# Letting a main product be issued up to ten places ahead of the first unissued one

## The chip, the cores and the metric

The program runs on one core of a Trainium2 chip. The metric is the device time of one execution in microseconds (us), the median of several. Below, PE is the matrix engine (TensorE), DVE the vector engine, ACT the scalar engine, POOL the general engine (GpSimd) and SP the engine whose queue issues all the DMAs here. Matmuls read SBUF and write PSUM, which here is eight banks of 128 partitions by 512 floats.

## The reference

Three layers in a row, all in float32, on 4 batches of 768 tokens (3072 tokens in all).

```python
# attention: 4 batches, 8 heads, 768 tokens, head size 64
scores = scale * np.matmul(q, k.transpose(0, 1, 3, 2))
keep = is_global | is_local            # 8 global keys, and the 96 keys up to the query's own
scores = np.where(keep, scores + bias, -1000000000.0)
a = exp(scores - max); a = a / (sum(a) + 1e-09)
x = (a @ v) as [3072, 512]
# layer 1: w_in [512, 2048], w_out [2048, 512]
h = x @ w_in;  x = (h * np.cos(h)) @ w_out
# layer 2: weights of the same shapes
h = np.maximum(x @ w_in, 0.0);  return h * h @ w_out
```

## The kernel before

**Tiling.** The 3072 tokens are cut into six blocks of 512 (`b` = 0 to 5), each of four tiles of 128 tokens. Every float32 operand of a large product is split into two float16 parts, high and low, and a product is the sum of three float16 products (`PRODS`). Attention goes tile by tile (`attend32` for the first four tiles, `attend` for the others), in two groups of four heads: scores (`scores_and_bias`, or bias by DVE for the last tiles), maximum, exponential, a transpose of the probabilities by DMA, and `values`, whose sums DVE divides (line 929) into `x`.

**The main products.** Layer 1 of a block is 16 steps `j`. `first(b, j)` (line 1038) multiplies the block's `x` with a 128-column part of `w_in` into one PSUM bank, 12 matmuls of 512 columns. `hidden` (ACT and DVE) turns the bank into the pair of halves `g` that `second(b, j)` (line 1056) multiplies with a row part of `w_out`, again 12 matmuls, added up over `j` in four other banks. Layer 2 is done with seven instead of eight products of quarters (`product`, line 1148: the names P1 to P7, 12 matmuls of 256 columns each), then `tokens` (line 1350) for blocks 0 to 2 and `second2` (line 1270) for blocks 3 to 5; for the latter `token_quarters` prepares the quarters. All these go through one helper, `pe` (line 1032). The PSUM banks are two pools of four: `h` for `first`, for P1 to P7, for the scores and for `values`; `yp` for the sums of `second`, `tokens` and `second2`.

**Weights.** They come as raw 64-bit words, 1 MB at a time, for two steps `j` each. `decoded` (line 486) turns them into float32 by one ACT and three DVE operations, `weight` (line 498) splits them, the low half on DVE or POOL (line 409). While block 0 is in layer 1 its weights are still being decoded, `w_in` and `w_out` in turn.

**The order of the work.** Nothing is issued by hand. Every piece of work is a `Work` object in a `Plan` with a cost in us, a due time, the buffers that it takes, and the pieces that it depends on. `order` first hands due times down: a piece is due no later than 0.01 us before each piece that depends on it. `run` then plays a clock: whenever an engine is free, it takes the piece with the earliest due time among those whose dependences are done and whose buffers can be had (`can_get`, which keeps buffers back for pieces that are due earlier). The result is one fixed list for each engine; on the chip each engine issues its list in that order and waits where an operand or a buffer is late.

**The row.** `pe` ties each main product to the one before it in the order in which the program writes them down: the predecessor is in `after`, so a main product isn't ready in the planner until its predecessor is done, whatever its own operands. That order is, in layer 1, `first(b, j)` followed by `second` of three steps earlier (`LAG = 3`), across the border of blocks too; in layer 2 the P products with `tokens` or `second2` between them (`fill`). The scores, the values and the norms of attention are added by `plan.add` directly and aren't in the row.

Of the kernel before, what the change touches and what calls it, by code (L numbers as in the profile page):

```python
# [79 lines left out]
SLACK = 0.8  # L80
SWITCH = 10.0
AHEAD_OF = 6
ROUNDS = 1


class Buf:
    def __init__(self, pool):
        self.pool, self.slot, self.users, self.writers, self.readers = pool, None, [], [], []
# [10 lines left out]
class Plan:  # L99
    def __init__(self, pools):  # L100
        self.free = {k: list(range(n)) for k, n in pools.items()}
        self.work = []

    def add(self, ways, due, emit, r=(), w=(), new=(), part=(), after=(), lag=0.1, tab=None):

# [25 lines left out]

    def order(self):

        for o in reversed(self.work):
            for d in o.deps:
                d.due = min(d.due, o.due - 0.01)
        for o in self.work:
            for d in sorted(o.deps, key=lambda d: d.n):
                d.outs.append(o)
        best = None  # L140
        self.ends = []
        for n in range(ROUNDS):
            try:
                started = self.run()
            except RuntimeError:
                if best is None:
                    raise
                break
            self.ends.append(round(self.end, 1))
            if best is None or self.end < best[0]:  # L150
                bufs = {b: b.slot for o in started for b in o.gets}
                best = self.end, started, [(o.start, o.end, o.eng) for o in started], bufs, self.switches
            self.relax(started, n)
        self.end, started, placed, bufs, self.switches = best
        for o, (o.start, o.end, o.eng) in zip(started, placed):
            pass
        for b, b.slot in bufs.items():
            pass
        return started
# [32 lines left out]
    def run(self):  # L192
# [4 lines left out]
        for o in work:  # L197
            o.left, o.eng = len(o.deps), None
            for b in o.bufs:
                users[b] = len(b.users)  # L200
        lines = {k: [] for k in pools}
        for o in sorted(work, key=lambda o: (o.due, o.n)):
            for b in o.gets:
                lines[b.pool].append(o)
# [4 lines left out]
        port_until, port_by, bus, table = 0.0, None, 0.0, "exp"  # L209
        events, now, done = [], 0.0, 0  # L210
# [11 lines left out]
        def can_get(o):  # L222
            need = {}
            for b in o.gets:
                need[b.pool] = need.get(b.pool, 0) + 1
            for p, k in need.items():
                line, i = lines[p], at[p]
                while line[i].eng is not None:
                    i += 1
                at[p] = i  # L230
                kept, seen = 0, 0
                while line[i] is not o:
                    if line[i].eng is None:
                        kept += 1
                        seen += 1
                        if seen > AHEAD_OF:
                            return False
                    i += 1
                if len(pools[p]) < k + kept:
                    return False  # L240
                if o.ways[0][0] == "SP" and pools[p][k - 1][0] > now + 1e-9:
                    return False
            return True

        while done < len(work):
            moved = True
            while moved:
                moved = False
                for e in engines:
                    if free_at[e] > now + 1e-9:  # L250
                        continue
                    if e == "SP" and bus > now + AHEAD:
                        seq += 1
                        heapq.heappush(events, (bus - AHEAD, 3, seq, None, None))
                        continue
                    held, pick, key = [], None, 0.0
                    beside = e == "DVE" and self.waits_for_pool(ready, free_at, now)
                    while ready[e]:
                        item = heapq.heappop(ready[e])
                        o = item[2]  # L260
                        if o.eng is not None:
                            continue
                        way = next(w for w in o.ways if w[0] == e)
                        port = way[2]
                        ok = can_get(o) and not (port and port_until > now + 1e-9 and port_by != e)
                        if ok and e == "POOL" and len(o.ways) > 1:
                            ok = self.pool_may(o, now, free_at, ready)
                        if ok and e == "ACT":
                            k = o.due + (SWITCH if o.tab not in (None, table) else 0.0)
                            if pick is None or k < key:  # L270
                                pick, key = (o, way), k
                            if key <= o.due:
                                held.append(item)
                                break
                        elif ok and e == "DVE":
                            k = o.due + (SHARED if len(o.ways) > 1 else 0.0) + (BESIDE if port and beside else 0.0)
                            if pick is None or k < key:
                                pick, key = (o, way), k
                            if key <= o.due:
                                held.append(item)  # L280
                                break
                        elif ok:
                            pick = (o, way)
                            break
                        held.append(item)
                        if len(held) > 60:
                            break
                    for item in held:
                        if pick is None or item[2] is not pick[0]:
                            heapq.heappush(ready[e], item)  # L290
                    if not pick:
                        continue
                    o, way = pick
                    o.eng, o.start = e, now
                    for b in o.gets:
                        b.slot = pools[b.pool].pop(0)[1]
                    if e == "SP":
                        issue, xfer = way[1]
                        end_issue = now + issue
                        bus = max(bus, end_issue) + xfer  # L300
                        end = bus + 1.8
                        free_at[e] = end_issue
                    else:
                        end = free_at[e] = now + way[1]
                        if e == "ACT" and o.tab not in (None, table):
                            table, end = o.tab, end + 1.3
                            free_at[e] = end
                            self.switches += 1
                        if way[2]:
                            port_until, port_by = end, e  # L310
                    o.end = end
                    seq += 1
                    heapq.heappush(events, (end + o.lag, 0, seq, o, None))
                    heapq.heappush(events, (free_at[e], 2, seq, None, None))
                    for x in o.outs:
                        same = e != "SP" and len(x.ways) == 1 and x.ways[0][0] == e
                        seq += 1
                        heapq.heappush(events, (end if same else end + o.lag, 1, seq, o, x))
                    started.append(o)
                    moved = True  # L320
# [8 lines left out]
            now = events[0][0]  # L329
            while events and events[0][0] <= now + 1e-9:  # L330
                _, kind, _, o, x = heapq.heappop(events)
# [29 lines left out]
def fast_path(ctx, tc, kq, vt, w, n_raw, out, meanwhile):  # L361
# [32 lines left out]
    plan = Plan({k: len(v) for k, v in slots.items()})  # L394
# [69 lines left out]
    start, now = {}, T0  # L464
# [14 lines left out]
    def unit_due(m, b, e, j):  # L479
        step = LEN[m, b] / (2 * NJ)  # L480
        return start[m, b] + (2 * j + 5 * e) * step
# [545 lines left out]


    yd = {}
    last_pe = [None]  # L1030

    def pe(due, us, fn, **k):

        o = plan.add((("PE", us, False),), due, fn, after=[last_pe[0]] if last_pe[0] else (), lag=0.3, **k)
        last_pe[0] = o
        return o

    def first(b, j, due):
# [540 lines left out]
    for m, b in SEQ:  # L1579
# [17 lines left out]
        for j in range(0 if m or b in SEVEN else NJ):  # L1597
            due = unit_due(0, b, 0, j)
# [11 lines left out]
        for q in range(0 if m or b not in SEVEN else NQ):  # L1610
            due = start[0, b] + q * LEN[0, b] / NQ
# [7 lines left out]
        for q in range(NQ if m else 0):  # L1619
            due = start[1, b] + q * LEN[1, b] / NQ  # L1620
# [257 lines left out]
```

## Time and profile before

| | us |
|---|---|
| median of 3 runs | 1136.92 |
| lowest and highest run | 1131.3 and 1138.05 |
| the profiled execution | 1133.71 |
| its span, first to last instruction | 1132.0 |
| PE busy in it | 1082.7 (96%) |
| DVE busy | 743.7 (66%) |
| ACT busy | 743.4 (66%) |
| POOL busy | 155.2 (14%) |
| mean granted clock of TensorE | 0.986 of full |

The span is a little shorter than the device time. Busy time counts an instruction from start to end; matmuls overlap one another by a little, so that a listed duration of 12 matmuls is longer than their share of a dense stream. A bracket behind a row, as `[1.58 <-DVE x L929]`, is the idle time of the engine before that instruction and what ended it.

### The profile page before, as it was taken

Reading aid. Unit: us, or ns where it says so; the run is one execution under the profiler, and the core shown is the slowest. Engines: PE = TensorE matmul, PEld = TensorE weight load, DVE = VectorE, ACT = ScalarE, POOL = GpSimd, SP = SyncE. Lnnn points to the kernel's source line nnn. Section 1 sums busy time; section 2 is a strip of 40 time slices with the busy share of each in tenths; the row PEclk is TensorE's granted clock in tenths of the full one; section 3 lists DMA queues with packets and bytes.
Section 4 is the critical chain, followed back from the end, with each engine's and each line's share of the span. In section 5 each row is a group of like instructions: output and inputs, shape, how many; then the busy total and the mean of one; then the engine's idle time right before and its main releaser. Section 6 shows DMA issues by size and latency. Waiting matters only on the chain.

```text
span 1132.0 us, 21315 instructions
## 1 busy us (share of the span) xinstructions
PE 1082.7 (96%) x8612; PEld 677.2 (60%) x8612; DVE 743.7 (66%) x1347; ACT 743.4 (66%) x1283; POOL 155.2 (14%) x125
## 2 busy tenths in 40 slices
PE   6898899989999999999999999999999999999997
PEld 5744444544455444666666554666544588888886
DVE  6998887569777975575554564455683277477473
ACT  6979767688999663775754865674554377376361
POOL 0211220012121210120000110000140032022010
PEclk9988989999999999999999999999999999999999
DMA  5576779449787873588786624586873363334201
GB/s 214 196 216 169 243 248 290 124 85 258 226 209 185 301 272 112 194 262 234 224 204 237 184 94 93 141 219 185 331 263 137 121 224 112 128 126 149 77 9 41
DMA packets 151979, 207.65 MB, mean 183 GB/s; under 512 B 103808, under 2 KB 104320, under 8 KB 150336
## 3 DMA queue, kind: packets, MB, share of 16 engines
q1 hardware_dynamic: 151872, 206.21, 60.0%
q8 instruction: 69, 1.13, 0.4%
q14 instruction: 38, 0.31, 0.1%
HBM read 149.03 MB, written 32.51 MB: 160 GB/s over the span
## 4 chain that ended last, share of the span: by engine, by line
PE 83%; DVE 10%; ACT 4%; DMA 1%; issue 1%; SPq 0%; POOL 0%; DVEq 0%; ACTq 0%; POOLq 0%
PE hps L1047 20%; PE ypps L1063 19%; PE hps L1154 18%; PE ypps L1360 11%; PE ypps L1290 7%; PE hps L912 2%; DVE nm L807 2%; PE hps L1290 2%; PE hps L851 1%; DVE dec L65 1%; DMA raw<-w 1%; ACT L815 1%; ACT e L815 1%; DVE p L409 1%; PE hps L1487 1%
## 5 line engine op out<-in xcount | busy, mean ns | idle before, releaser
L1047 PE MATMUL hps<-xy,w 128*128 128x512 f16 x1152 | 273.4, 388 | 10.5 <-ACT e L815 3.2
L1063 PE MATMUL ypps<-g,ld 128*128 128x512 f16 x1152 | 264.6, 379 | 0.6 <-issue 0.4
L1154 PEld LDWEIGHTS <-ld 128*128 128x128 f16 x2016 | 196.1, 98 | 35.5 <-issue 4.0
L1047 PEld LDWEIGHTS <-w 128*128 128x128 f16 x1152 | 111.9, 99 | 146.3 <-issue 17.2
L1154 PE MATMUL hps<-ys,ld 128*128 128x256 f16 x1680 | 196.4, 273 | 1.4 <-ACT t L1390 1.4
L1063 PEld LDWEIGHTS <-ld 128*128 128x128 f16 x1152 | 112.6, 98 | 135.3 <-issue 1.7
L409 DVE TENSOR_TENSOR g<-t,g 128x512 f16<-128x512 f32 x142 | 109.3, 771 | 50.3 <-ACT g L1131 49.7
L1348 DVE TENSOR_TENSOR t<-hps,t 128x512 f32<-128x512 f32 x120 | 82.7, 689 | 88.9 <-PE hps L1154 87.9
L1360 PE MATMUL ypps<-ld,g 128*128 128x512 f16 x576 | 133.2, 379 | 0.0
L1087 DVE SCALAR_TENSOR_TENSOR t<-t,hps 128x512 f32<-128x512 f32 x96 | 65.6, 683 | 87.2 <-ACT t L1085 87.0
L1131 ACT ACTIVATE g<-t 128x512 f16<-128x512 f32 x144 | 90.0, 625 | 39.9 <-DVE t L1087 38.4
L1083 ACT ACTIVATE t<-hps 128x512 f32<-128x512 f32 x96 | 57.1, 594 | 86.4 <-PE hps L1047 83.7
L1360 PEld LDWEIGHTS <-g 128*128 128x128 f16 x576 | 55.8, 98 | 57.6
L1345 ACT ACTIVATE t<-t 128x512 f32<-128x512 f32 x72 | 45.0, 625 | 61.5 <-DVE t L1348 61.4
L1085 ACT ACTIVATE t<-t 128x512 f32<-128x512 f32 x96 | 60.4, 629 | 2.7
L1180 ACT ACTIVATE t<-t 128x512 f32<-128x512 f32 x96 | 60.3, 629 | 2.6
L409 DVE TENSOR_TENSOR p<-e,p 128x1024 f16<-128x1024 f32 (+1 forms) x32 | 37.3, 1167 | 31.0 <-ACT p L899 30.9
L1345 ACT ACTIVATE t<-hps 128x512 f32<-128x512 f32 x24 | 14.3, 597 | 50.4 <-PE hps L1154 50.3
L875 DVE CUSTOM_DVE_ANT_0 e<-hps,bias 128x256 f32<-128x256 f32 (+2 forms) x96 | 31.7, 387 | 18.4 <-PE hps L851 18.3
L883 ACT ACTIVATE e<-e,nm 128x256 f32<-128x256 f32 (+1 forms) x96 | 39.1, 477 | 3.6 <-DVE nm L875 3.5
L65 DVE SCALAR_TENSOR_TENSOR dec<-raw,dec 128x1024 int32<-128x1024 int32 x32 | 40.3, 1258 | 0.6
L409 POOL TENSOR_TENSOR kq<-ld,kq 128x1024 f16<-128x1024 f32 x9 | 19.9, 2211 | 149.9 <-ACT kq L628 149.9
(193 smaller groups left out, 1515.7 us busy)
## 6 DMA issues: line engine op xcount, KB each, us to landing
ld<-w SPq DMA_DIRECT2D x146, 512.0 KB, 4.2
raw<-w SPq DMA_DIRECT2D x32, 1024.0 KB, 5.5
w<-ld SPq DMA_DIRECT2D x36, 512.0 KB, 3.0
ld<-kq SPq DMA_DIRECT2D x23, 512.0 KB, 5.2
ld<-vt SPq DMA_DIRECT2D x24, 256.0 KB, 3.3
yd<-xy SPq DMA_DIRECT2D x6, 1024.0 KB, 6.1
xy<-yd SPq DMA_DIRECT2D x6, 1024.0 KB, 5.6
ld<-w SPq DMA_DIRECT2D x24, 256.0 KB, 3.6
```

The source lines that it names most:

```text
L409: op.emit = lambda: eng[op.eng].tensor_tensor(out=out_f(), in0=src_f(), in1=hi_f(), op=ALU.subtract)
L1047: nc.tensor.matmul(out=at(ps), lhsT=w_view(wt)[:, a, j % 2, k * 128:(k + 1) * 128], rhs=x_view(src)[:, c, k, :], start=(n == 0), stop=(n = ...
L1063: nc.tensor.matmul(out=at(y_ps[d]), lhsT=wv[:, a, d * 128:(d + 1) * 128], rhs=at(g)[:, c], start=(j == 0 and n == 0), stop=(j == NJ - 1 an ...
L1085: act(due + 1.2, 512, lambda: nc.scalar.activation(out=at(t), in_=at(t), func=ACTF.Square, scale=HALF_TURN), w=[t])
L1087: dve(due + 1.9, 0.7, lambda: nc.vector.scalar_tensor_tensor(out=at(t), in0=at(t), scalar=-S_X / S_H, in1=at(ps), op0=ALU.add, op1=ALU.mul ...
L1131: act(due, 512, lambda: nc.scalar.activation(out=at(g)[:, 0], in_=at(t), func=ACTF.Copy), r=[t], new=[g])
L1154: nc.tensor.matmul(out=at(bank)[:, 256 * u:256 * u + 256], lhsT=wv(a, u, kk), rhs=sv(c, kk), start=(fresh and u == n == 0), stop=(last and ...
L1180: act(due, 512, lambda: nc.scalar.activation(out=at(t), in_=at(t), func=ACTF.Square), w=[t])
L1290: nc.tensor.matmul(out=at(bank)[:, 256 * half:256 * half + 256], lhsT=gv(home)[:, z, c0:c0 + 128], rhs=wv(a, u), start=(q == half == u == ...
L1345: act(due, 512, lambda: nc.scalar.activation(out=at(t), in_=at(ps), func=ACTF.Relu, scale=ROOT), **k)
L1348: dve(due, 0.7, lambda: nc.vector.tensor_tensor(out=at(t), in0=at(bank), in1=at(u), op=ALU.add), port=False, **k)
L1360: nc.tensor.matmul(out=at(y_ps[d]), lhsT=at(g)[:, z, 256 * u + d % 2 * 128:256 * u + d % 2 * 128 + 128], rhs=wv[:, a, u], start=(q == i == ...
```

## The change

The predecessor is no longer a dependence. `pe` only notes each main product in `plan.row`. `order` still hands due times down along the row, as if the dependence were there, so due times still rise along it. In `run`, a new test `may_pass` lets a main product be taken when its place in the row is at most ten (`PASSING`) beyond the first one that isn't issued; other work isn't touched by it. All true dependences, those by buffers, stay.

```diff
+PASSING = 10
...
-        self.work = []
+        self.work, self.row = [], []
...
+        before = dict(zip(self.row[1:], self.row))
         for o in reversed(self.work):
-            for d in o.deps:
+            for d in (*o.deps, *([before[o]] if o in before else ())):
                 d.due = min(d.due, o.due - 0.01)
...
+        rank = {o: i for i, o in enumerate(self.row)}
+        stands = [0]
+
+        def may_pass(o):
+            i = rank.get(o)
+            if i is None:
+                return True
+            while self.row[stands[0]].eng is not None:
+                stands[0] += 1
+            return i - stands[0] <= PASSING
+
...
-                        ok = can_get(o) and not (port and port_until > now + 1e-9 and port_by != e)
+                        ok = can_get(o) and not (port and port_until > now + 1e-9 and port_by != e) and may_pass(o)
...
-    last_pe = [None]
 
     def pe(due, us, fn, **k):
 
-        o = plan.add((("PE", us, False),), due, fn, after=[last_pe[0]] if last_pe[0] else (), lag=0.3, **k)
-        last_pe[0] = o
+        o = plan.add((("PE", us, False),), due, fn, lag=0.3, **k)
+        plan.row.append(o)
         return o
```

## Rows read from the trace of the kernel before

**Rows 1.** The page, its parts 1 and 2: busy shares, and clock by fortieths
```profile
PE 1082.7 (96%) x8612; PEld 677.2 (60%) x8612; DVE 743.7 (66%) x1347; ACT 743.4 (66%) x1283; POOL 155.2 (14%) x125
PEclk9988989999999999999999999999999999999999
```

**Rows 2.** Busy time by stage: stretch, its length, busy us of each engine, clock, DMA
```profile
92.00:126.00 34.00, 28.13 (x224) 14.07 (x223) 30.89 (x43) 28.42 (x48) 10.31 (x6) 0.88 0.71 205
126.00:160.00 34.00, 29.37 (x193) 13.54 (x191) 29.01 (x35) 25.96 (x37) 5.89 (x4) 0.87 0.85 245
160.00:181.00 21.00, 17.96 (x147) 8.54 (x146) 19.73 (x28) 14.79 (x21) 1.16 (x1) 1.00 0.75 255
181.00:310.00 129.00, 123.41 (x1045) 63.67 (x1043) 90.62 (x187) 105.67 (x170) 17.20 (x10) 1.00 0.68 188
310.00:838.00 528.00, 527.81 (x3999) 302.87 (x3998) 328.22 (x618) 345.12 (x583) 60.46 (x37) 1.00 0.69 205
905.00:1020.00 115.00, 109.63 (x992) 96.60 (x991) 81.53 (x149) 72.19 (x132) 27.85 (x26) 1.00 0.43 148
1124.00:1132.00 8.00, 0.42 (x4) 0.13 (x2) 2.08 (x6) 0.00 (x0) 0.00 (x0) 0.76 0.20 73
```

**Rows 3.** PE in order of time, 97 to 181 us: start, length, instruction, idle before
```profile
101.94 0.40 PE L800 MATMUL hps<-bias,ident 128*128 128x192 bf16 x2 [3.68 <-DVE x L929]
103.03 5.01 PE L1047 MATMUL hps<-xy,w 128*128 128x512 f16 x12
...
123.78 0.38 PE L800 MATMUL hps<-bias,ident 128*128 128x448 bf16 x2 [1.84 <-DVE t L1087]
...
142.54 1.04 PE L1047 MATMUL hps<-xy,w 128*128 128x512 f16 x2 [1.96 <-ACT w L503]
...
167.47 2.33 PE L1063 MATMUL ypps<-g,ld 128*128 128x512 f16 x10 [0.26 <-DVE ld L409]
169.64 2.75 PE L1047 MATMUL hps<-xy,w 128*128 128x512 f16 x12
...
180.43 2.75 PE L1047 MATMUL hps<-xy,w 128*128 128x512 f16 x12 [2.78 <-ACT e L815]
```

**Rows 4.** DVE, POOL and SP in order of time: last operands of weights and x
```profile
95.28 1.23 DVE L409 TENSOR_TENSOR ld<-dec,ld 128x1024 f16<-128x1024 f32 x1
...
130.48 1.23 DVE L409 TENSOR_TENSOR ld<-dec,ld 128x1024 f16<-128x1024 f32 x1 [0.46 <-ACT ld L503]
...
157.09 2.13 POOL L409 TENSOR_TENSOR w<-dec,w 128x1024 f16<-128x1024 f32 x1 [2.25 <-ACT w L503]
...
162.03 1.24 SPq L1024 DMA_TRANSPOSE xy<-g  x1
...
173.21 1.21 DVE L409 TENSOR_TENSOR ld<-dec,ld 128x1024 f16<-128x1024 f32 x1
```

**Rows 5.** PE, then DVE, in order of time, 200 to 253 us
```profile
201.37 0.38 PE L800 MATMUL hps<-bias,ident 128*128 128x512 bf16 x1 [0.95 <-DVE norms L1491]
...
231.28 0.89 PE L912 MATMUL hps<-v,pt 128*128 128x65 f16 x24 [1.58 <-DVE x L929]
...
252.78 0.89 PE L912 MATMUL hps<-v,pt 128*128 128x65 f16 x24 [1.58 <-DVE x L929]
...
215.84 0.69 DVE L409 TENSOR_TENSOR g<-t,g 128x512 f16<-128x512 f32 x1 [0.69 <-ACT g L1131]
...
241.12 0.69 DVE L409 TENSOR_TENSOR g<-t,g 128x512 f16<-128x512 f32 x1 [0.31 <-ACT g L1131]
```

**Rows 6.** PE in order of time, 905 to 1020 us, layer 2 of blocks 3 to 5
```profile
910.09 2.78 PE L1154 MATMUL hps<-ys,ld 128*128 128x256 f16 x24 [0.63 <-ACT t L1390]
...
938.82 2.78 PE L1154 MATMUL hps<-ys,ld 128*128 128x256 f16 x24 [0.73 <-ACT t L1390]
...
1015.65 2.78 PE L1154 MATMUL hps<-pt,ld 128*128 128x256 f16 x24 [1.48 <-ACT t L1390]
...
1019.56 1.38 PE L1290 MATMUL ypps<-w,kq 128*128 128x256 f16 x11 [0.95 <-POOL kq L409]
```

## The prediction

> **What bounds the kernel now.** I read the page's first two parts, then busy time by stage, then PE in order of time in the stages where it idles, then the other engines at the idle moments. PE is busy 96% of the span and no other engine over 66% [rows 1], so only PE's idle time and its time at the lower clock can be won. The stage table says where these are [rows 2]. From 310 to 838 us PE idles 0.19 us in 528: nothing to win. The end, from 1124, is 8 us of gathering and writing out behind the last matmul; no main product is left to move. That leaves three stretches: A, 92 to 181, where the rows give 34 - 28.13, 34 - 29.37 and 21 - 17.96, together 13.5 us idle, and granted clocks of 0.88 and 0.87; B, 181 to 310, 5.6 us idle; C, 905 to 1020, 5.4 us idle. Before 92 the row can't help much: no main product has a ready companion until x and the first weights are there.
>
> **What the change removes and adds.** It adds no instruction, no DMA and no semaphore of its own; the same 8612 matmuls run [rows 1]. It removes one reason for PE to stand still in the planner's clock. Due times still rise along the row, so the list differs from the old one only where the first unissued product can't go while a later one can. Call the steps f_j and s_j (`first` and `second`). s_j writes the yp banks, f_j an h bank, so an s_j can go when the h banks are all held by attention. With each product its followers move too: for an s none until the last of a block, whose output copies and 1 MB store come one product earlier at most; for an f the ACT and DVE work of `hidden`. A product is 12 matmuls: ten take 169.64 - 167.47 = 2.17 us, so twelve 2.60 [rows 3].
>
> **Stretch A.** Summed idle time is a trap here. PE stands before s12 until 167.47 because its weights are being split (0.26 us of waiting shown) [rows 3], and f14, two steps earlier, needed weights that POOL finished at 157.09 + 2.13 = 159.2 [rows 4]. So the decoding sets the pace: PE has caught up with it at 167.5, and an earlier gap is worth something only if what fills it leaves another ready product for the time until 167.5. The gaps of 3.68 and 1.84 us at 98 and 122, where a score waits for an h bank, and of 1.96 at 140 [rows 3] could each take a second: s4 had its weights at 95.28 + 1.23 = 96.5, s9 at 131.7 [rows 4], and their g were older. But PE then has one product less to do at 160 to 167, and one that could move in is f0 of block 1, whose x left by its transpose at 162.03 + 1.24 = 163.3 plus the landing [rows 4] and which now starts at 169.64 [rows 3]. That makes one product, 2.60. The second is s14: its weights were complete at 173.21 + 1.21 = 174.4 [rows 4], PE idles 2.78 us until 180.43 for an h bank for f1 of block 1 [rows 3], and s14 stands behind that f1 in the row. That is another 2.60. A gives 5.2 of 13.5; the bounds are 0 (both filled by work that attention then pays for) and 7.5.
>
> The clock: the 12 matmuls at 103.03, after the 3.68 us gap, are listed at 5.01 us instead of 2.75 [rows 3], which is 1.2 instead of 2.4 GHz for nearly all of them. In A that time lies ahead of the point where PE has caught up with the weights anyway, so I take 0 of it; the upper bound, 5.01 - 2.75 = 2.3 us, is what makes 7.5 of 5.2. The Trainium skill, page "TensorE: Matmul & The Clock Gate", section "HAM oscillation — how this bites in real kernels", says that a wait between bursts lets the engine fall back to half rate, so that the next burst starts cold. The trace agrees in the pair of rows at 101.94 and 103.03. By that rule a filled gap would pay twice, and the sum would be 2.3 us lower.
>
> **Stretch B.** At 231.28 and 252.78 `values` waits 1.58 us for the bank that the division of the group before it releases, and at 201.37 a score waits 0.95 [rows 5]. Each time seconds lie ready behind an f that needs a bank too: before 231 s5 of block 1 with its g from 215.84 + 0.69 = 216.5, before 253 s8 with its g from 241.8 [rows 5]. These waits come from the order of bank use and the planner sees them in its own clock. A second of 2.60 closes each gap, and the values start up to 2.60 - 1.58 = 1.0 us late, which their followers (division, copy, transpose) can bear while products lie ready. I take 0.95 + 2 x 1.58 = 4.1 of 5.6; bounds 0 and 5.6.
>
> **Stretch C.** At 910.09, 938.82 and 1015.65 PE waits 0.63, 0.73 and 1.48 us for ACT's copy of P1's bank before P2 may add to it [rows 6]; P5 or a `second2` stands behind and may now go. Sum 2.84; since P5 needs another h bank and DVE is 71% busy here [rows 2], I take half, 1.4; bounds 0 and 2.84. The 0.95 at 1019.56 is another kind: the product's first matmul ran and its second operand, the low half from POOL, was late [rows 6]. The planner believed it ready, and passing can't see it.
>
> **What it costs.** Passed products can hit that same lateness: issued as soon as the planner thinks an operand done. Nothing in the trace before shows it for a passed product; the nearest row is that 0.95 us [rows 6]. With some ten passes I take two such waits, 1.9 us; bounds 0 and ten, 9.5. The other engines' orders shift a little; from 310 to 838 they are covered by PE's backlog, ACT being busy 345 and DVE 328 of 528 us [rows 2].
>
> **Sum.** 5.2 + 4.1 + 1.4 - 1.9 = 8.8 us less, on the profiled execution 1133.7 - 8.8 = 1124.9. That execution lies 3.2 us under the median of the runs, 1136.9; half of this is added, since either may be the typical one: 1126.5, that is 0.9% under the median.
>
> **Rivals.** *The gaps only move* (decoding and banks set the pace, seconds taken early are missing at the next gap). For it: A, where 8.3 of the 13.5 us are already explained so. Then only half of B and C are left, about 3 us: 1133. *More than that*: all bounds on the good side, 7.5 + 5.6 + 2.8 = 15.9, nothing lost: 1133.7 - 15.9 + 1.6 = 1119.4. For it: the ready times in rows 4 and 5 are 2 to 15 us before the gaps. *Nothing changes*: the planner, whose costs differ from the chip's, sees none of these gaps and writes the same list: 1136. Against it: the waits in rows 5 are alike to 0.01 us and follow from bank counts.
>
> *Slower*: the products stand in attention's way. PE's list is strict, so a 2.60 us product taken into a shorter gap delays the score or the values that would have ended it. In the Trainium skill, the same page, section "The mechanism", matmuls start and end in program order and only weight loads are pulled ahead; the trace agrees, the products at 103.03 and 180.43 standing behind their waits. Place: the eight groups of tiles 4 to 7, two PE pieces each, that make x of block 1. If each of 16 pieces met a fresh product, half of it on average, 1.3 us, x would be 21 us later; 169.64 less 163.3, some 6 us, is spare, so it decides from five such meetings on. Then 15 us are lost, two more products at half clock cost 2 x 2.3, and B and C still give 3.6 net of their waits: 1135.3 (the mean of median and profile) + 15 + 4.6 - 3.6 = 1151. Against it: the buffers are kept for earlier due work, and a product passes only when nothing due earlier can go.
>
> **Chances.** About 1% is what a measurement of this kernel can tell from no change. The forecast (1126.5, a little inside 1%) has 0.38, split evenly across the border at 1125.6; gaps only move 0.20; more 0.17; no change 0.11; slower 0.14, of which 0.01 stays within 1%. Faster by over 1%: 0.19 + 0.17 = 0.36; within: 0.19 + 0.20 + 0.11 + 0.01 = 0.51; slower 0.13. The range takes in the second, third and fourth rival and their spread, 1117 to 1141; the slower case and a piece of the best one stay outside, some 0.17.
>
> **What would show it.** In the changed profile, s14 of block 0 runs before f1 of block 1 near 178; the 1.58 us waits before `values` are gone or shorter; PE's busy time is unchanged up to the clock while its idle time from 92 to 310 falls from 19 to about 10 us. Wrong would be: new waits of `second` or `second2` on POOL or DVE results of over 2 us in sum, the first product of block 1 later than 169.6, or idle time between 310 and 838, where there was none.

## The result, and the profile after

Before 1135.35 us (median of 4 runs, 1131.3 to 1138.05), after **1114.38 us** (4 runs, 1112.89 to 1115.46): ratio 0.9829, 95% interval 0.9808 to 0.9851. The profiled execution took 1113.74 us, its span 1112.0. The gain is some 20 us where 8.8 were forecast, and 1114.4 lies under the low end of the range, 1117.

The page of the kernel after, its span, busy shares and clock by fortieths, against [rows 1]:

```profile
span 1112.0 us, 21314 instructions
PE 1077.9 (97%) x8612; PEld 676.5 (61%) x8612; DVE 738.1 (66%) x1341; ACT 734.9 (66%) x1279; POOL 159.2 (14%) x131
PEclk9989989999999999999999999999999999999999
```

The same 8612 matmuls; PE is busy 4.8 us less, and the span is 20.0 us shorter, so 15.2 us are idle time.

Busy time by stage of the kernel after, columns as in [rows 2] (stretch, its length, busy us of PE, PEld, DVE, ACT, POOL, clock, DMA share, GB/s):

```profile
92.00:126.00 34.00, 29.14 (x224) 14.58 (x222) 30.98 (x45) 28.57 (x48) 4.75 (x3) 1.00 0.73 205
126.00:160.00 34.00, 28.84 (x174) 13.01 (x174) 30.75 (x34) 26.39 (x39) 11.66 (x6) 0.85 0.85 255
160.00:181.00 21.00, 21.00 (x182) 10.75 (x180) 17.77 (x23) 13.37 (x22) 2.13 (x1) 1.00 0.80 263
181.00:310.00 129.00, 129.00 (x1106) 66.26 (x1105) 93.29 (x192) 111.72 (x186) 26.09 (x17) 1.00 0.71 190
310.00:838.00 528.00, 527.63 (x3966) 302.12 (x3959) 332.78 (x635) 338.67 (x575) 55.82 (x35) 1.00 0.69 211
905.00:1020.00 115.00, 114.52 (x1050) 102.49 (x1048) 82.13 (x152) 72.50 (x134) 34.16 (x33) 1.00 0.38 128
```

B and the stretch from 160 have no idle time left, C has 0.48 us, and A still has 4.86 + 5.16 = 10.0. From 92 to 310 idle time fell from 19.1 to 10.0 us, about as forecast (A and B by themselves came out otherwise, see below); the rest of the gain is somewhere else.

To find it I counted, in both traces, the matmuls issued up to a moment, each at its time in a stream at 2.4 GHz: the **lead** is the work by which PE of the kernel after is ahead at the same time of the span.

| at us | lead, us | gained in | forecast (bounds) |
|---|---|---|---|
| 90 | 0 | | |
| 180 | 6.9 | A: 6.9 | 5.2 (0 to 7.5) |
| 310 | 13.3 | B: 6.4 | 4.1 (0 to 5.6) |
| 905 | 13.5 | | 0 |
| 1020 | 19.8 | C: 6.3 | 1.4 (0 to 2.84) |
| end | 20.0 | cost: none outside A | -1.9 (-9.5 to 0) |

PE in order of time in the kernel after, from A, B and C:

```profile
109.22 4.92 PE L1059 MATMUL hps<-xy,w 128*128 128x512 f16 x22 [3.04 <-DVE w L422]
...
141.05 0.60 PE L1059 MATMUL hps<-xy,w 128*128 128x512 f16 x2 [1.88 <-DVE dec L68]
143.39 7.53 PE L1059 MATMUL hps<-xy,w 128*128 128x512 f16 x22 [1.73 <-DVE w L422]
...
162.74 5.34 PE L1075 MATMUL ypps<-g,ld 128*128 128x512 f16 x24
167.92 2.75 PE L1059 MATMUL hps<-xy,w 128*128 128x512 f16 x12
...
171.88 4.06 PE L1075 MATMUL ypps<-g,ld 128*128 128x512 f16 x18
...
177.81 2.75 PE L1059 MATMUL hps<-xy,w 128*128 128x512 f16 x12
...
242.45 1.63 PE L925 MATMUL hps<-v,pt 128*128 128x65 f16 x48
...
891.69 9.33 PE L1166 MATMUL hps<-ys,ld 128*128 128x256 f16 x84
900.86 1.47 PE L1302 MATMUL ypps<-raw,kq 128*128 128x256 f16 x12
```

`first` is now line 1059, `second` 1075, the P products 1166, `second2` 1302. At 242.45 the 48 matmuls of two groups of values run as one, where [rows 5] had 1.58 us between such groups. At 171.88 seconds fill the time in which [rows 3] stood still before 180.43. At 891.69 seven P products run in a row ahead of the first `second2`. The price of passing is to be seen too: firsts wait for weights at 109.22, 141.05 and 143.39, 6.65 us in sum. No first passed anything there: seconds that stood between the firsts were issued earlier, so the firsts come up one behind another.

**Idle time under-reports a gap.** Twelve matmuls of 512 columns are listed at 2.75 us and twenty-four at 5.34, so one in a stream takes (5.34 - 2.75) / 12 = 0.216 us, and the last of a group is listed at 2.75 - 11 x 0.216 = 0.38. Ahead of a gap this last one shows 0.16 us as busy that a stream would have used for the next. So each closed gap gives its idle time and 0.16 us. The Trainium skill, page "TensorE: Matmul & The Clock Gate", sections "Single matmul latency" and "Back-to-back issue gap", gives (398 + N) / 2.4 ns for a single matmul and N / 2.4 + 2.5 ns from one to the next, 379 and 216 at 512 columns: the trace agrees with both. The 131 ns that the second section gives for a sustained stream of such matmuls isn't seen here; the stream takes 216. B: its 5 gaps, 5.59 us, all closed: 5.59 + 5 x 0.16 = 6.4, the lead measured. C: six of its seven gaps closed, 4.9 + 6 x 0.16 = 5.9 of the 6.3.

### The profile page after: what moved, and what is told of

The parts are those of the page before. It is cut to its first block, busy times and chain, and to the rows that moved or that the text cites. A ratio compares the mean times of both kernels' runs of the same rounds, so it can differ in the third digit from the quotient of the medians.

```text
span 1112.0 us, 21314 instructions
## 1 busy us (share of the span) xinstructions
PE 1077.9 (97%) x8612; PEld 676.5 (61%) x8612; DVE 738.1 (66%) x1341; ACT 734.9 (66%) x1279; POOL 159.2 (14%) x131
## 4 chain that ended last, share of the span: by engine, by line
PE 93%; DVE 5%; ACT 1%; DMA 1%; issue 0%; SPq 0%; DVEq 0%; ACTq 0%
PE hps L1059 22%; PE ypps L1075 22%; PE hps L1166 20%; PE ypps L1372 11%; PE ypps L1302 8%; PE hps L925 2%; PE hps L864 2%; PE hps L1302 2%; PE ypps L761 1%; DVE dec L65 1%; PE hps L879 1%; PE hps L733 1%; PE hps L1499 1%; PE hps L813 1%; DVE dec L68 1%; DMA ld<-kq 1%
## 5 line engine op out<-in xcount | busy, mean ns | idle before, releaser
L1059 PE MATMUL hps<-xy,w 128*128 128x512 f16 x1152 | 269.7, 386 | 9.2 <-DVE w L422 4.8
L1166 PEld LDWEIGHTS <-ld 128*128 128x128 f16 x2016 | 196.2, 98 | 32.3 <-issue 0.7
L422 DVE TENSOR_TENSOR g<-t,g 128x512 f16<-128x512 f32 x138 | 103.2, 748 | 53.5 <-ACT g L1143 52.9
L422 POOL TENSOR_TENSOR p<-e,p 128x1024 f16<-128x1024 f32 (+1 forms) x14 | 28.2, 2015 | 239.6 <-ACT p L912 207.6
L65 DVE SCALAR_TENSOR_TENSOR dec<-raw,dec 128x1024 int32<-128x1024 int32 x32 | 43.7, 1367 | 0.6
L422 DVE TENSOR_TENSOR p<-e,p 128x1024 f16<-128x1024 f32 (+1 forms) x26 | 30.2, 1160 | 20.6 <-ACT p L912 18.9
L422 POOL TENSOR_TENSOR g<-t,g 128x512 f16<-128x512 f32 x18 | 23.2, 1292 | 138.3 <-ACT g L1143 112.7
```

The source lines that it names most:

```text
L422: op.emit = lambda: eng[op.eng].tensor_tensor(out=out_f(), in0=src_f(), in1=hi_f(), op=ALU.subtract)
L1059: nc.tensor.matmul(out=at(ps), lhsT=w_view(wt)[:, a, j % 2, k * 128:(k + 1) * 128], rhs=x_view(src)[:, c, k, :], start=(n == 0), stop=(n = ...
L1166: nc.tensor.matmul(out=at(bank)[:, 256 * u:256 * u + 256], lhsT=wv(a, u, kk), rhs=sv(c, kk), start=(fresh and u == n == 0), stop=(last and ...
```

## The experiments

All are edits of the changed kernel. Ratios are against the kernel before, with 95% intervals; leads are of the profiled executions.

**Where the gain is: three parts of the row.** Each main product notes the layer and block of the loop in which the program writes it down, and only those of some blocks may pass.

```diff
+    zone = [None]
...
+        plan.tag[o] = zone[0]
...
     for m, b in SEQ:
+        zone[0] = (m, b)
...
-            return i - stands[0] <= PASSING
+            return i - stands[0] <= (PASSING if self.tag[o] == (0, 0) else 0)
```

> The changed kernel, but only main products that block 0 writes down in layer 1 may pass. Theory (each stage gains by its own passes): PE is 6.9 us of work ahead of the kernel before by 180 us of the span, half of it because the half-clock stretch at 101 to 108 us is gone (6.8 us at half rate, worth 3.4), and this lead is kept to the end: 1128 to 1129 against 1135 (ratio 0.994). Rival (the passes of block 0 only move its gaps, and the lead at 180 comes from passes of block 1): lead under 3 us at 180, ratio 0.998 or more.

Measured: 1130.05 us, 0.9954 (0.9936 to 0.9972), by the ratio 5.2 us less. The lead is 3.9 at 170, 5.7 at 180, and 3.7 from 310 on: a new stretch at 1.2 GHz, from 197.6 to 201.1, takes some of it back. Block 0 gives 3.7 to 5.7 us; s14 isn't in it, since it is written down in block 1's loop.

```diff
-            return i - stands[0] <= PASSING
+            return i - stands[0] <= (PASSING if self.tag[o] in [(0, 1), (0, 2), (0, 3)] else 0)
```

> The changed kernel, but only main products of blocks 1 to 3 in layer 1 may pass. Theory: the 1.58 us waits ahead of the values and the waits at 201 and 306 us go, each worth its idle time and the 0.16 us by which a last matmul is listed longer than its share, 6.4 us in all: 1129, ratio 0.994; the half clock at 101 to 108 us stays. Rival (lateness of attention takes part of it back, as the prediction had it): 4 us or less, ratio 0.9965 or more.

Measured: 1124.88 us, 0.991 (0.9892 to 0.9928), by the ratio 10.2 us less. The lead goes from -1.7 at 170 to 7.3 at 400, which is 9.0: the 6.4 of B and the 2.6 of s14. Busy time by stage, this kernel:

```profile
181.00:310.00 129.00, 129.00 (x1092) 66.45 (x1091) 92.80 (x195) 109.54 (x184) 16.73 (x11) 1.00 0.68 192
```

B has no idle time although nothing passes in block 0 or in layer 2: this part stands by itself.

```diff
-            return i - stands[0] <= PASSING
+            return i - stands[0] <= (PASSING if self.tag[o] in [(1, 2), (1, 3), (1, 4), (1, 5)] else 0)
```

> The changed kernel, but only main products of layer 2 of blocks 2 to 5 may pass; up to 838 us the order is that of the kernel before. Theory: the waits at 905 to 1020 us go by passes made there, 6.3 us: 1129, ratio 0.9945. Rival (the lead that the earlier stages give is what fills this stage, and its own passes are worth 1.4 us as predicted): 1134, ratio 0.9985.

Measured: 1127.69 us, 0.9939 (0.9918 to 0.9961), by the ratio 6.9 us less. C alone gives 9.4 - 3.2 = 6.2 us of lead. That the bound of 2.84 holds is refuted. The 3.2 that this kernel had at 905 stand at 310 already (3.3), and its order is that of the kernel before up to 750 us (not 838, as was expected): they come from what TensorE's clock did in A.

By their ratios the three parts give 5.2 + 10.2 + 6.9 = 22.3 us and the whole change 19.4; within the intervals they add up.

**Which passes make C.** The tag is now the pool of the PSUM bank that the product writes: `h` for firsts and P products, `yp` for `second`, `tokens` and `second2`.

```diff
+        plan.tag[o] = o.bufs[-1].pool
...
-            return i - stands[0] <= PASSING
+            return i - stands[0] <= (PASSING if self.tag[o] == 'h' else 0)
```

> The changed kernel, but only products that write an h bank may pass (the first products of layer 1, P1 to P7, and the last block's final products), none that writes a yp bank. Theory: stages A and B are filled by seconds, which write yp, so they stay as before; stage C is filled by P products that pass a waiting P2 or a second product of layer 2: 6.3 us, all in 905 to 1020, ratio 0.9945, and the waits there for a low half from POOL go with it, because the second products come later. Rival (C is filled by second products passing P2): no gain there, ratio 0.999 or more.

Measured: 1127.47 us, 0.9948 (0.9927 to 0.9968). The lead grows by 6.1 in C, so it is P products that pass there. What PE waited for between 905 and 1020, first in the kernel before, then in this one (us in total, times, longest):

```profile
PE hps L1154 <- ACT t L1390: 2.8, 3, 1.5
PE ypps L1290 <- POOL kq L409: 1.9, 2, 1.0
PE hps L1154 <- DVE t L1348: 0.5, 1, 0.5
PE ypps L1290 <- DVE kq L409: 0.2, 1, 0.2
```

```profile
PE hps L1167 <- DVE t L1361: 0.5, 1, 0.5
```

Not only the 2.8 of the copies is gone, but the 2.1 of the low halves that `second2` reads. Why, the POOL rows and then PE's rows of this experiment show (start, length, instruction):

```profile
937.93 1.16 POOL L422 TENSOR_TENSOR kq<-t,kq 128x512 f16<-128x512 f32 x1
```

```profile
935.92 5.40 PE L1167 MATMUL hps<-ys,ld 128*128 128x256 f16 x48
941.16 1.47 PE L1167 MATMUL hps<-pt,ld 128*128 128x256 f16 x12
942.47 1.47 PE L1167 MATMUL hps<-ys,ld 128*128 128x256 f16 x12
943.78 1.47 PE L1303 MATMUL ypps<-w,kq 128*128 128x256 f16 x12
```

The half is ready at 937.93 + 1.16 = 939.09 and read from 943.78 on, behind six P products. In the kernel before it was ready at 941.52 + 1.16 = 942.68, and the product that reads it had begun at 941.49, behind two P products:

```profile
941.52 1.16 POOL L409 TENSOR_TENSOR kq<-t,kq 128x512 f16<-128x512 f32 x1 [1.78 <-ACT kq L1264]
```

```profile
938.82 2.78 PE L1154 MATMUL hps<-ys,ld 128*128 128x256 f16 x24 [0.73 <-ACT t L1390]
941.49 0.28 PE L1290 MATMUL ypps<-w,kq 128*128 128x256 f16 x1
942.73 1.38 PE L1290 MATMUL ypps<-w,kq 128*128 128x256 f16 x11 [0.95 <-POOL kq L409]
```

```diff
-            return i - stands[0] <= PASSING
+            return i - stands[0] <= (PASSING if self.tag[o] == 'h' == self.tag[self.row[stands[0]]] else 0)
```

> The kernel in which only writers of an h bank may pass, and now only when the first unissued product writes an h bank too: P5 may pass a waiting P2, but no P product may pass a second product of layer 2. Theory (the two kinds of passes in 905 to 1020 us work together: a P past P2 closes the waits on ACT's copy, but brings the second products behind it to PE sooner, so their waits for low halves grow): the ACT waits of 2.8 us go, the waits before second products grow from 2.2 to 3 us or more, net 2 us or less of the 6.2, ratio 0.998 or more. Rival (the terms add up, each gap closed by its own pass): 3.3 us, ratio 0.997, the waits on low halves staying at 2.2.

Measured: 1137.45 us against 1133.65, 1.0033 (1.0016 to 1.005): a little **slower**. P products pass one another, but not the `second2` that stands between them. What PE waited for, 890 to 1060:

```profile
PE ypps L1303 <- ACT kq L1277: 4.3, 2, 2.4
PE ypps L1303 <- DVE kq L422: 1.2, 3, 0.4
PE hps L1167 <- DVE t L1361: 0.5, 1, 0.5
```

The copies of P1's bank are waited for no longer, and `second2` waits 5.5 us for its operands instead of 2.1. The wait moved to the next piece of the row and grew, from 5.4 to 6.0 us in all. That is the smaller part of the loss. A stretch at 1.2 GHz came with it, 1022.0 to 1025.4, which costs half its length, 1.7 us; and over all runs the mean granted clock is 0.984 here and 0.987 before, where 0.001 goes with about 1 us (last section).

```diff
-            return i - stands[0] <= PASSING
+            return i - stands[0] <= (PASSING if self.tag[o] == 'h' != self.tag[self.row[stands[0]]] else 0)
```

> The other half: writers of an h bank may pass only when the first unissued product writes a yp bank, so P products may pass a waiting second product of layer 2, but P5 may not pass P2. Theory: the waits for low halves (2.2 us) go, the waits for ACT's copy (2.8 us) stay or grow; net 1 to 3 us, ratio 0.9975 or more, so that e5 and e6 together stay 2 us or more under the 6.2 that both kinds give at once. Rival (the terms add up): 2.9 us here, 6.2 in sum.

Measured: 1131.31 us, 0.9985 (0.9968 to 1.0002); lead in C 2.8. What PE waited for, 905 to 1020:

```profile
PE hps L1167 <- ACT t L1403: 2.8, 3, 1.5
PE hps L1167 <- DVE t L1361: 0.5, 1, 0.5
```

The mirror image: the low halves are in time, the copies are waited for as before. By ratios the two kinds of passes give +0.33% and -0.15% (which may be nothing), and together -0.52%. Between 890 and 1060 PE waits 5.4 us in the kernel before, 6.0 and 3.3 with one kind of pass and 0.5 with both. So they need one another.

```diff
-            return i - stands[0] <= PASSING
+            return i - stands[0] <= (PASSING if self.tag[o] == 'yp' else 0)
```

> The complement of the kernel in which only writers of an h bank may pass: only writers of a yp bank may (seconds, tokens, second products of layer 2). Theory: the lead to 838 us is that of the changed kernel, 12 to 14 us; in 905 to 1020 us idle time is not less than the 5.4 us of before, since no P product can be pulled ahead of a waiting second product: 1121 to 1122, ratio 0.989. Rival (the lead makes the last stage's waits vanish by itself): 1115, ratio 0.983.

Measured: 1120.7 us, 0.9891 (0.9874 to 0.9909). The lead is about 13 at 400 and still 13.0 at 1020: seconds taken early make the whole of A and B, and next to nothing of C (4.72 us of idle time, 5.37 before). Up to 498 us its order on PE is that of the changed kernel, so up to there no first passes anything in that one either. Busy time, this kernel:

```profile
905.00:1020.00 115.00, 110.28 (x1002) 97.69 (x1001) 79.70 (x149) 70.14 (x128) 24.34 (x22) 1.00 0.37 127
```

```diff
-PASSING = 10
+PASSING = 1
```

> The changed kernel with 1 instead of 10 places. Theory (in layer 1 the one second behind a waiting first product is what fills, in layer 2 a product must get past several second products): the lead at 838 us is 10 us or more, in 905 to 1020 us nothing is won or some is lost: 1121 to 1126, ratio 0.989 to 0.993. Rival (one place is enough everywhere): 1116 or less, ratio 0.984.

Measured: 1127.28 us, 0.9933 (0.991 to 0.9957), a little above what was expected. One place is enough for A and B (lead 13.4 at 840) and harmful in C, where it falls to 6.7 at 1040. What PE waited for, 905 to 1045:

```profile
PE ypps L1302 <- ACT kq L1276: 3.7, 2, 1.9
PE ypps L1302 <- POOL g L422: 1.9, 2, 0.9
PE ypps L1302 <- DVE kq L422: 0.9, 2, 0.4
PE hps L1166 <- DVE t L1360: 0.5, 1, 0.5
PE hps L1166 <- ACT t L1402: 0.4, 2, 0.2
```

The same move of the wait as in the slower kernel above: 6.5 us before `second2`, and 1.2 GHz from 931.5 to 934.9 and from 1010.0 to 1013.4, which is some 3.4 of the 6.7 us of lead that are lost.

**What holds A back.** Ten us of idle time are left in A. The prediction said that the decoding of the weights sets the pace there.

```diff
-            dve(due - 5.6 + 1.3 * n, us, lambda n=n: join_steps(nc, at(t), r())[n](), r=[raw] if n else [], w=[t])
+            cut = 8 if m == 0 and n == 2 else 1024
+            dve(due - 5.6 + 1.3 * n, us, lambda n=n, cut=cut: join_steps(nc, at(t)[:, 0:cut], r()[:, 0:cut])[n](),
+                r=[raw] if n else [], w=[t])
```

> The changed kernel with the same order on every engine, but the third decoding step of layer 1's weights (the sign bits) is done for 8 of 1024 columns, so each of 16 DVE operations of 1.2 us before 180 us falls to under 0.2; the signs of these weights are left out. Theory (from 92 to 167 us the decoding on DVE sets the pace, which is why only 2 products' worth of the 13.5 us of idle time could be won there): the 10 us of idle time left in 92 to 160 us fall by half or more, with some half-clock time; 1104 to 1109, ratio 0.973 to 0.978 against before. Rival (PSUM banks and attention set the pace there): under 2 us less than the changed kernel, 0.981 or more.

Measured: 1112.92 us, 0.9812 (0.9792 to 0.9832), some 2 us under the changed kernel, idle time from 92 to 160 at 8.5 us instead of 10.0. DVE's time for this step alone doesn't set the pace; the other two steps and the low halves were left on DVE.

```diff
+        part = 128 if m == 0 and jj > 1 else 1024
...
-            out=r().rearrange("p (u a) b -> p u (a b)", u=2),
-            in_=w[m, e, 2 * jj:2 * jj + 2].bitcast(INT32).rearrange("u p c -> p u c")), new=[raw])
+            out=r().rearrange("p (u a) b -> p u (a b)", u=2)[:, :, 0:part],
+            in_=w[m, e, 2 * jj:2 * jj + 2].bitcast(INT32).rearrange("u p c -> p u c")[:, :, 0:part]), new=[raw])
```

> The changed kernel with the same order, but the raw weights of layer 1 from the third pair of steps on (12 of 16 loads) are read for an eighth of their columns, 128 KB instead of 1 MB; the rest of those weights is stale. The cheaper third decoding step alone moved the time by about 2 us, so DVE's time isn't what paces the decoding. Theory now (the two raw buffers and the landing of their loads do): the idle time of 92 to 160 us falls from 10 to 5 us or less, and the time to 1104 to 1109. Rival (the places in the lists do: loads and joins are issued behind attention's work, whatever they last): 1111 or more.

Measured: 1114.96 us, 0.9821 (0.9795 to 0.9847), no gain over the changed kernel. DMA busy from 126 to 160 falls from 0.85 to 0.56, and PE waits for weights as before, 4.3 and 2.6 us. The landing of the loads alone doesn't set it either.

```diff
+        part = 128 if m == 0 and jj > 1 else 1024
...
+            cut = 8 if m == 0 else 1024
...
```

> As the kernel with short loads, and all three decoding steps of layer 1's weights on DVE for 8 of 1024 columns as well; the weights are wrong by that. Theory (loads and joins form one loop through two raw buffers, so that only both together open it): idle time of 92 to 160 us under 3 us, 1102 to 1107. Rival (attention's own chain and its PSUM banks hold PE up at these points): 5 us of idle time or more stay, with waits on ACT's exponentials or on the transposes in place of those on weights.

Measured: 1109.17 us, 0.9774 (0.9749 to 0.9799), 5 to 6 us under the changed kernel. All three steps are short here and one was in the first of these runs, so it isn't shown that it takes short loads and short steps together. 7.6 us of idle time stay from 92 to 160: neither theory had it so. What PE waited for, 92 to 181:

```profile
PE hps L1062 <- ACT w L519: 2.5, 1, 2.5
PE hps L1062 <- DVE w L422: 1.8, 2, 0.9
PE hps L816 <- ACT e L831: 1.7, 1, 1.7
PE hps L928 <- DMA pt<-p: 1.3, 1, 1.3
PE hps L1062 <- POOL w L422: 0.3, 1, 0.3
```

The chain of work that ended last, followed from 92 to 160 us (68 us with the ends of its first and last pieces), says where the pace went. In the changed kernel 32.3 us of it are DVE's, 17.6 of these the three decoding steps, and 6.0 ACT's. Two of its pieces are:

```profile
119.47 2.97 DVE dec L65
...
131.27 3.03 DVE dec L65
```

In this last run 7.5 us are DVE's and 25.5 ACT's; ACT kept its own step of the decoding. So a chain over DVE's whole list, decoding and attention, becomes one over ACT's. Whether relieving both would win the rest was not tried.

The last run leaves the decoding alone and puts `second` four steps behind `first` in the row instead of three, so that more seconds are ready when attention or a weight is late:

```diff
-    LAG = 3
+    LAG = 4
```

> The changed kernel with the second products written down four steps after their first instead of three (LAG = 4), a version that may beat both: one more ready second lies in stock when first products wait. Theory: stage 92 to 180 us wins one product more, 2.6 us, the rest as in the changed kernel: 1110 to 1112, ratio 0.979 to 0.981. Rival (the stock isn't what is missing there, as s products wait for decoded weights too): no gain, 0.983.

Measured: **1108.4 us** (1107.91 to 1109.84), 0.9769 (0.9744 to 0.9794): better than both kernels, 6 us under the changed one. From 92 to 181 it has 3.3 us less idle time than the changed kernel and 3.4 us less at 1.2 GHz, worth 1.7. Busy time by stage:

```profile
92.00:126.00 34.00, 31.51 (x258) 16.14 (x255) 31.68 (x48) 31.17 (x52) 9.41 (x7) 1.00 0.88 262
126.00:160.00 34.00, 30.45 (x190) 13.94 (x190) 30.66 (x31) 24.69 (x38) 12.77 (x7) 0.90 0.82 232
```

Idle time from 92 to 160 is 6.0 us, and the lead over the kernel before is 8.0 at 110 and 12.1 at 180, where the changed kernel has 4.3 and 6.9. The decoding moved along. Issues of the raw loads on SP's queue, the fourth and the sixth of the stretch behind 92 us, in the kernel before, in the one after, and in this one:

```profile
129.66 0.52 SPq L490 DMA_DIRECT2D raw<-w  x1
...
148.04 0.38 SPq L490 DMA_DIRECT2D raw<-w  x1
```

```profile
125.64 0.38 SPq L503 DMA_DIRECT2D raw<-w  x1
...
144.06 1.14 SPq L503 DMA_DIRECT2D raw<-w  x1
```

```profile
121.33 0.38 SPq L503 DMA_DIRECT2D raw<-w  x1
...
138.54 3.49 SPq L503 DMA_DIRECT2D raw<-w  x2
```

The loads start 4 us earlier with the change and 8 to 10 us earlier with the longer lag. So the decoding isn't a clock that runs by itself: when it starts moves with PE's order and with the lists of the other engines, which the planner changes along with it. Through which buffer or which list it does was not tried alone.

## Why the prediction was wrong

**The direction and the places were right.** The waits of 1.58 us are gone, seconds fill the time before f1 of block 1 at 177.81, the first product of block 1 isn't late (167.92 at the latest, against 169.64 in [rows 3]), 310 to 838 stays without idle time (0.37 us), and idle time from 92 to 310 falls by 9.1 us, where the sum had 5.2 + 4.1. That this last number agrees is luck: it is 3.5 in A and 5.6 in B. No new wait of `second` or `second2` over 2 us in sum came up; it was firsts that met new waits. The slower rival is refuted: x of block 1 was in time.

**C is the step that failed, and the largest miss, 4.9 of 11 us.** The prediction took 1.4 and a bound of 2.84, and of the 0.95 us for the low half it said that it "is another kind" and "passing can't see it". It looked at which wait a passing product can fill, and not at what passing does to the pieces that it passes. P products that go early put work between the making of the half and its use; the half is then in time. The runs show it both ways: P past `second2` alone takes away the 2.1 us for the halves and leaves the 2.8 for the copies, P past P alone takes away the copies and makes `second2` wait 5.5 us. Only both give the 6.2 us, and with one place C loses. I also halved the term "since P5 needs another h bank"; no new wait for a bank shows.

**B was sized 2.3 us too low**, 4.1 instead of 6.4. I left out two of its five gaps, 1.09 us before 306.27 and 0.39 before 202.98, though the stage row in [rows 2] has all 5.6 of them; and 5 x 0.16 us of matmul time that a gap hides in the busy column. The bound, 5.6, was the idle time and so too low for the same reason.

**The cost was put at 1.9 and is nothing outside A.** It was priced as passed products that meet late operands; no such wait shows. In A firsts meet late weights, 6.65 us, but they passed nothing: with s4 and s5 issued before f7, the firsts f7, f8 and f9 follow one another, and f8 stands for its weights until 109.22. That is what the rival "the gaps only move" said, and of a part of A it is true. PE stood in A before as well, and the stage's idle time falls from 13.5 to 10.0 all the same: 3.5 us, less than the two products of 5.2.

**A's sum came out near, 6.9 for 5.2, by luck, with other terms.** The gaps gave 3.5 us and four fewer of them 0.65. The remainder, about 2.8, is the clock: the stretch at 1.2 GHz from 100.8 to 107.6 in the trace before isn't there after (0.88 in [rows 2], 1.00 now). The prediction took 0 of it and 2.3 as its bound. One pair of traces can't settle the size: kernels with the order of before up to 750 us or more lead it by -0.6 to 3.3 us at 310, with nothing changed there but the clock. Together the runs can. All six kernels that keep the gap of 3.68 us (98 to 102 in the kernel before) fall to 1.2 GHz between 100.4 and 103.0, none of the eight that fill it does; and the mean granted clock is 0.987 over 48 runs of the kernel before and 0.989 over 26 runs of five that fill it (the changed one, block 0 alone, `yp` alone, the lighter third step, the short loads). At about 1 us for each 0.001 that is some 2.5 us. Between the two traces, the 20 us less 6.2 for C and 6.4 for B leave 7.4 for A with s14.

**The premise in A fell.** "The decoding sets the pace: PE has caught up with it at 167.5" read a moment in which PE waited as a limit that holds whatever PE does. A second in stock brings PE 5 us further by 180 with the same decoding work, 1.7 of it by the clock. The decoding does weigh: it is 17.6 of the 32.3 us that DVE has in the chain. But no run shows what the remaining 6 to 7 us of A hang on; the chains point to DVE's list as a whole, and behind it to ACT's.

**The range** ended at 1117 since the best case added bounds that were themselves too low: 15.9 instead of 6.9 + 6.4 + 6.3 = 19.6. The rival "more than that" was the right one; its price, 1119.4, was the three bounds.

## What to carry to other kernels

When work may go out of turn, price not only the wait that it fills: everything that it passes starts later, and its operands get that much more time. Where pieces take turns along a chain, allow it to all of them, since a wait that is taken from one piece can come back larger at the next (of 5.4 us of waits one half of the passes left 6.0, the other 3.3, both together 0.5). A bound from idle time needs 0.16 us more for each gap of TensorE, and half of a stretch at 1.2 GHz where one follows the gap. A stage of late operands isn't a fixed pace until a run shows that it doesn't move with the order.

## What the runs showed of the hardware

**A gap doesn't always bring the lower clock.** After the gap of 3.04 us at 109.22 the 22 matmuls took 4.92 us, 0.22 each, the pace of 2.4 GHz; after the two shorter ones at 141.05 and 143.39 the same number took 7.53. The Trainium skill, page "TensorE: Matmul & The Clock Gate", section "HAM oscillation — how this bites in real kernels", tells of a kernel in which bursts start cold after waits of some 3 to 5 us. At the gap of 3.68 us before 101.94 [rows 3] all six kernels that have it agree with that. At the place of the 3.04 us, four kernels with that gap (the changed one, block 0 alone, `yp` alone, short loads) stayed at 2.4 GHz, and the one with the lighter third step fell to 1.2 from 109.5 to 112.9 after only 1.99. So the length of a gap doesn't tell by itself, and a closed gap pays twice only where the trace shows the lower clock behind it.

**The same order falls to 1.2 GHz at different places.** Up to 310 us, three kernels with one order were at the lower clock at 100.8 to 107.6, 124.7 to 128.1 and 141.7 to 148.6 (before), at 100.6 to 107.4 and 138.2 to 145.0 (passes in layer 2 alone), and at 102.9 to 109.7 and 143.8 to 147.2 (`h` alone), beside one at the start of each. Their leads over the first at 310 us are 3.3 and 0.9 us. The kernel before spreads over 1129.7 to 1138.6 us in 48 runs, and most of that goes with this clock: the 14 runs with a mean granted clock of 0.985 or less took 1136.1 to 1138.6 us, the 11 with 0.989 or more 1129.7 to 1132.8, about 1 us for each 0.001. Around that line 0.9 us of scatter are left of 2.3. What makes the same order fall more or less often is not shown.
